# Dilated heads first, larger first loads, a value copy that may go to ScalarE, and slot sums copied out in two parts

## The chip, the cores and the metric

The kernel runs on one core of a Trainium2 chip. Its engines are TensorE (PE, with weight loads shown apart as PEld), VectorE (DVE), ScalarE (ACT), GpSimd (POOL) and SyncE (SP); 16 DMA engines move data. The metric is the device time of one launch in microseconds. Three runs of the kernel before took 178.34, 179.11 and 179.09 us, a median of 179.09.

## The reference: what is computed

Attention over 8 batches, 8 heads, 576 positions and 64 features, then a soft mixture of 8 experts with 4 slots each, over the 4608 tokens of 512 features that attention gives. Heads 0 to 3 see a plain window, heads 4 to 7 a dilated one:

```python
scores = scale * np.matmul(q, k.transpose(0, 1, 3, 2))
rel = pos[:, None] - pos[None, :]
mask_plain = (rel >= 0) & (rel < 32)
mask_dil = (rel >= 0) & (rel < 128) & (rel % 4 == 0)
masks = [mask_plain if h < H // 2 else mask_dil for h in range(H)]
attn = softmax(where(masks, scores, -1e9)); out = attn @ v
# x: the tokens, 4608 x 512
logits = x @ phi                                   # 32 slots
d = exp(logits - max over tokens), normalized over tokens
slot_input = d.T @ x                               # 8 experts x 4 slots
h = np.maximum(slot_input[e] @ w1[e], 0.0); slot_out[e] = h @ w2[e]
c = exp(logits - max over slots), normalized over slots
result = c @ slot_out
```

All inputs and the result are float32 in HBM. The result has 9.4 MB; the inputs read have 61.9 MB.

## The kernel before, in words

**Units.** Attention is cut into 8 units. A unit is two batches and either the four plain heads or the four dilated ones; units 0, 2, 4, 6 are plain and units 1, 3, 5, 7 dilated (`ty = u % 2`). Units 2k and 2k+1 are the two halves of the heads of batches 2k and 2k+1.

**Loads.** POOL issues all loads, since they turn float32 into bfloat16. A unit's q, k and v go to one of three staging buffers `stg` (32 partitions each for q, k and v). A dilated unit takes three commands (L417), each row one piece of 9216 elements; a plain unit takes six (L424), each row two pieces of 4608 elements. The first unit is loaded in two halves (`load_first`, L438), each in six commands with pieces of 2304 elements, so that its first transposes need not wait for the whole. The load of unit u+3 waits until PE has transposed unit u out of its buffer. The weights of the first layer (`w1`) go to `WD` and one buffer of `stg`; those of the second (`w2`) go to the three `stg` buffers and then to `TT` when the last units are done with them. The last two to use `stg` (`wpair`, L806) are cut into row groups with tiny extra transfers (`mk`, L787) between them. The last weights (L473) are cut by halves of their 512 columns.

**A unit's stages.** `st_T` (L566): PE transposes q, k, v (plain: 144 of 64 rows by 96, L582; dilated: 72 of 128 rows by 96, L577) and ACT copies them to `TT` (L603). `st_S` (L610): PE computes scores (L621), ACT their exponentials into `PT` (L628), DVE multiplies by the mask (L636); six blocks. `st_V` (L639): PE turns v back (L646) and DVE copies it to `VN` (L651), four times. `st_P`: PE multiplies (L675), DVE takes the reciprocal of the sums (L684) and scales into `XB` (L686), four times. `st_X`: PE transposes `XB` (L703), DVE or ACT copies it to `XT` (L715, L716), whichever the planner finds free first.

**A pair's stage.** After the second unit of a pair, `st_L` does for each batch: logits (L730), their exponential with its sum over tokens `csum` (L735), re-ordered pieces `expX` (L742), a transpose by a selecting matrix (L761), its copy `ET` (L765), and the slot sums into a PSUM bank `psA` (L774).

**The end.** DVE copies `psA` out (L854); PE folds it in two parts of two blocks each (L861), which become `siT` (L869); then the first layer (L883), ReLU (L890, L893), transposes (L901) and their copies, the sums over slots (L930), and the second layer (L957), by column halves at its end as the weights land. Each half is scaled (`so_sb`, L991), multiplied with the tokens' weights (L1009, L1022), scaled and stored by SP in 256-column pieces for six groups; four larger groups (L1072) follow with all 512 columns.

**What sets the order.** Each operation is recorded with its inputs, an estimated cost and a due time (`key`); a planner (`schedule`) places them on the engines, each engine in order, and writes the semaphores. Where PE would idle, it inserts matmuls of ones (L1090), the fillers, by the table `FILL` (times, modes, slack). POOL's and SP's commands keep the order in which they were recorded.

Of the kernel before, what the change touches and what calls it, by code (L numbers as in the profile page):

```python
# [8 lines left out]
ACTF = mybir.ActivationFunctionType  # L9
# [10 lines left out]
CT = 72  # L20
NU = 8
QB = 96
HALO = 32
FILL = ((1.5, 9.0, "h", 0.4, 0.43), (9.5, 13.5, "h", 0.6, 0.25), (13.5, 116.0, "h", 0.3, 0.216),
        (13.5, 24.0, "rf", 0.3, 0.216), (116.0, 143.0, "hrfc", 0.15, 0.216))
# [280 lines left out]
def bass_dilated_sliding_attn__then__soft_moe_slots_kernel(  # L306
# [12 lines left out]
    op = P.op  # L319
# [7 lines left out]
    stg = sb("stg", [128, 3, 9216])  # L327
# [21 lines left out]
    psA_sb = sb("psA_sb", [128, DM], F32)  # L349
# [29 lines left out]
    def sbt(t):  # L379
        return t.pool.ts[t.phys[0]]  # L380
# [7 lines left out]
    def bankb(t):  # L388
        return psb[:, t.phys[0], :]
# [8 lines left out]
    b_id0, b_id, b_sel, b_fold, b_rowm, b_phist, b_phi = [Buf() for _ in range(7)]  # L398
    b_acc, b_psA, b_csum, b_rcs, b_rtok = [Buf() for _ in range(5)]
    b_expT, b_expX = [Buf() for _ in range(B)], Buf()  # L400
# [4 lines left out]
    def due(u, x):  # L405
        return u * PACE + x

    def load_unit(u):
        bp, ty, s = u // 2, u % 2, u % 3

# [21 lines left out]
    def load_first(h_):  # L432
        def f(g):
            res = []
            for t, src in enumerate((q, k, v)):
                for bpar in range(2):
                    rows = src[bpar].rearrange("h (p c) d -> (h p) (c d)", c=CT)[0:32]
                    res.append(g.dma_start(  # L438
                        stg[32 * t + bpar:32 * t + 32:2, 0, :].rearrange(
                            "r (x f) -> r x f", x=2)[:, :, 2304 * h_:2304 * h_ + 2304],  # L440
                        rows.rearrange("(x r) f -> r x f", x=2)[:, :, 2304 * h_:2304 * h_ + 2304]))
            return res
        op("pool", f, w=[b_half[h_]], cost=3.5, sem=DmaSem(nc, f"s_first{h_}"),
           nbytes=96 * 4608 * 4, ndma=6)

# [110 lines left out]
    def win(u, t, h01, i, bpar):  # L556

        if u % 2 == 0:
            base = (2 * t + h01) * S + QB * i
        else:  # L560
            base = (4 * t + 2 * (i // 3) + h01) * 288 + QB * (i % 3)
        base -= HALO if t else 0
        n = QB if t == 0 else 128
        return TT[:, u % 2, 2 * base + bpar:2 * (base + n - 1) + bpar + 1:2]

    def st_T(u, j):  # L566
        ty, s = u % 2, u % 3
        src = stg[0:96, s, :].rearrange("r (x c d) -> r x c d", x=2, c=CT)
# [41 lines left out]
    def st_S(u, i):  # L610
        ty = u % 2
        sc, pt = tile(psum, 2), tile(pPT)
# [26 lines left out]
    def st_V(u, g):  # L639
# [4 lines left out]
        def pe(t):  # L644
# [5 lines left out]
        op("pe", pe, r=[b_id, b_TT[u % 2]], w=[pv], alloc=[pv, vn], cost=0.35, key=k0)  # L650
        op("dve", lambda dv: dv.tensor_copy(  # L651
            sbt(vn)[:, :, :, 0:64],
            bankb(pv)[:, 0:768].rearrange("p (m x d) -> p m x d", m=6, x=2)),
           r=[pv], w=[vn], cost=0.47, key=k0 + 0.6)

    def st_P(u, g):
        bp, ty = u // 2, u % 2
        bpar, h01 = g // 2, g % 2
# [32 lines left out]
    def st_X(u, bpar, x):  # L691
        bp, ty = u // 2, u % 2
        b = 2 * bp + bpar
# [448 lines left out]
```

## Time and profile before

| what | us |
|---|---|
| median of three runs | 179.09 |
| profiled execution: span from its first to its last instruction | 176.3 |
| first loads land (first half of unit 0) | 9.34 |
| first scores begin on PE (L621) | 16.99 |
| last unit transposed, POOL goes on | 116.73 |
| slot sums copied out (L854) | 134.20 |
| last weights landed, last second-layer matmuls begin | 152.17 |

Busy shares of the span: PE 80%, PEld 58%, DVE 64%, ACT 53%, POOL 24%. The page gives the profiled execution's own time as its span alone; the timed runs include what lies around it.

The page's first part is busy time of each engine; its second part cuts the span into 40 slices of 4.4 us, with one digit for each (9 is 90% or more), and gives for DMA the mean busy share of the 16 DMA engines and the GB/s that they moved. GB/s counts what is written: a load that turns float32 into bfloat16 reads twice that. A table of stretches gives for each stretch its length, each engine's busy time with its number of instructions, the granted clock of PE, the DMA share and GB/s. The share can be above 1, since an engine may have two pieces under way. The chain that ended last is followed back from the last instruction to what released it; its lines give start, length and what ran. In the timeline the bracket at the end of a line tells how long the engine had idled and for what. A DMA issue's line ends with the time from the command to its landing, with all the time that it stood in the queue.

### The profile page before, as it was taken

The page shows a single profiled execution, that of the slowest core. Times are in us where ns is not written, and L with a number is a line of the kernel's source. Part 1 is how long each engine was busy: PE and PEld are TensorE (multiplying, and loading weights), DVE is VectorE, ACT ScalarE, POOL GpSimd, SP SyncE. Part 2 cuts the span into 40 slices and gives each one's busy share as a digit, 9 for nine tenths or more (in the row PEclk, how much of TensorE's full clock was granted, in tenths as well). Part 3 has the DMA queues.
Part 4 walks back from the last instruction along what each step waited for, and adds up shares of the span by engine and source line. Part 5 has one row for each costly group of instructions (what it writes and reads, how often), then busy time and mean ns, then how long its engine had stood idle before and what let it go on. Part 6 is the DMA issues. An engine that isn't in the chain of part 4 may idle for free.

```text
span 176.3 us, 5745 instructions
## 1 busy us (share of the span) xinstructions
PE 141.8 (80%) x2574; PEld 101.4 (58%) x2574; DVE 113.6 (64%) x264; ACT 93.3 (53%) x143; POOL 42.4 (24%) x80
## 2 busy tenths in 40 slices
PE   7689988797989889797988698889899997598000
PEld 2266677566778667576966676776556555352000
DVE  6830986992897699479589467869953023489200
ACT  2044867744767866665885467577240212599000
POOL 7997105202200800500200010059930000000000
PEclk9969999999999999999999789999999999969955
DMA  4999999998999999999999999999999999999997
GB/s 71 178 230 206 207 217 210 234 225 185 224 207 219 240 209 196 215 213 214 239 200 211 214 218 214 216 218 214 216 207 214 205 193 200 268 344 398 448 428 297
DMA packets 12712, 40.80 MB, mean 231 GB/s; under 512 B 2256, under 2 KB 8912, under 8 KB 9424
## 3 DMA queue, kind: packets, MB, share of 16 engines
q0 software_dynamic: 8272, 30.94, 87.9%
q1 hardware_dynamic: 4416, 9.50, 14.0%
q8 instruction: 20, 0.33, 0.7%
q14 instruction: 4, 0.03, 0.0%
HBM read 61.93 MB, written 9.44 MB: 405 GB/s over the span
## 4 chain that ended last, share of the span: by engine, by line
PE 36%; DVE 21%; DMA 17%; POOL 7%; ACT 7%; issue 4%; POOLq 0%; DVEq 0%
DMA TT<-in_moe_w_dram 13%; PE ps L582 8%; DVE PT L636 6%; DVE XB L686 6%; PE ps L577 5%; ACT PT L628 4%; PE ps L703 4%; PE ps L730 4%; DVE VN L651 3%; DMA stg<-in_v_dram 3%; PE ps L646 3%; PE ps L621 3%; DVE WD L991 3%; PE ps L675 2%; PE ps L1090 2%
## 5 line engine op out<-in xcount | busy, mean ns | idle before, releaser
L603 ACT ACTIVATE TT<-ps 128x864 f32<-128x864 f32 x32 | 28.6, 896 | 28.4 <-PE ps L582 19.4
L628 ACT ACTIVATE PT<-ps 128x768 bf16<-128x768 f32 x48 | 36.7, 814 | 8.5 <-PE ps L621 8.4
L686 DVE TENSOR_TENSOR XB<-ps,RV 96x768 bf16<-96x768 f32 x32 | 30.3, 947 | 0.6
L651 DVE COPY VN<-ps 128x768 bf16<-128x768 bf16 x32 | 17.5, 546 | 6.4 <-PE ps L646 6.2
L1090 PE MATMUL ps<-wrm 128*128 128x512 bf16 x60 | 19.7, 458 | 1.1 <-DVE wrm L490 1.1
L582 PE MATMUL ps<-ident,stg 96*64 96x96 bf16 x576 | 16.5, 216 | 4.1 <-DMA stg<-in_v_dram 2.0
L715 DVE COPY XT<-ps 128x576 bf16<-128x576 bf16 x19 | 11.4, 598 | 12.8 <-PE ps L703 12.6
L675 PE MATMUL ps<-VN,PT 128*128 128x65 bf16 x384 | 17.8, 194 | 1.5 <-DVE PT L636 0.8
L582 PEld LDWEIGHTS ps<-ident,stg 96*64 96x64 bf16 x576 | 14.3, 116 | 7.6 <-DMA stg<-in_v_dram 2.6
L703 PE MATMUL ps<-ident,XB 96*128 96x96 bf16 x192 | 13.2, 207 | 4.9 <-DVE XB L686 2.9
L675 PEld LDWEIGHTS ps<-VN,PT 128*128 128x128 bf16 x384 | 14.5, 98 | 3.8 <-DVE PT L636 1.6
L646 PE MATMUL ps<-ident,TT 128*128 128x128 bf16 x192 | 16.0, 221 | 0.6 <-DVE VN L651 0.4
L621 PE MATMUL ps<-TT 64*128 64x96 bf16 x384 | 14.9, 204 | 1.2 <-ACT PT L628 0.9
L577 PE MATMUL ps<-ident,stg 96*128 96x96 bf16 x288 | 15.0, 206 | 0.5 <-DVE XB L686 0.3
L992 ACT ACTIVATE WD<-ps,rtok 128x256 f32<-128x256 f32 (+1 forms) x22 | 10.2, 559 | 8.4 <-PE ps L1009 8.2
L703 PEld LDWEIGHTS ps<-ident,XB 96*128 96x128 bf16 x192 | 9.7, 98 | 8.3 <-DVE XB L686 5.2
L577 PEld LDWEIGHTS ps<-ident,stg 96*128 96x128 bf16 x288 | 13.1, 98 | 0.7 <-DVE XB L686 0.4
L636 DVE TENSOR_TENSOR PT<-PT,mask_d 128x768 bf16<-128x768 bf16 x24 | 12.9, 546 | 0.7 <-ACT PT L628 0.2
L646 PEld LDWEIGHTS ps<-ident,TT 128*128 128x128 bf16 x192 | 10.8, 98 | 4.2 <-issue 1.3
L621 PEld LDWEIGHTS ps<-TT 64*128 64x128 bf16 x384 | 9.5, 94 | 5.8 <-ACT PT L628 2.3
L636 DVE TENSOR_TENSOR PT<-PT,mask_p 128x768 bf16<-128x768 bf16 x24 | 12.7, 539 | 0.1
L730 PE MATMUL ps<-XT,phi_pad 128*128 128x192 bf16 (+1 forms) x64 | 10.3, 306 | 1.6 <-issue 1.3
(95 smaller groups left out, 183.4 us busy)
## 6 DMA issues: line engine op xcount, KB each, us to landing
WD<-in_moe_w_dram POOLq DMA_DIRECT2D x7, 1024.0 KB, 30.6
stg<-in_moe_w_dram POOLq DMA_DIRECT2D x5, 1024.0 KB, 25.6
stg<-in_q_dram POOLq DMA_DIRECT2D x4, 576.0 KB, 22.0
stg<-in_k_dram POOLq DMA_DIRECT2D x4, 576.0 KB, 24.0
stg<-in_v_dram POOLq DMA_DIRECT2D x4, 576.0 KB, 26.8
out_dram<-WD SPq DMA_DIRECT2D x9, 256.0 KB, 2.8
out_dram<-WD SPq DMA_DIRECT2D x2, 1024.0 KB, 5.7
out_dram<-WD SPq DMA_DIRECT2D x1, 2048.0 KB, 9.2
```

The lines of the kernel that those rows point to most:

```text
L577: i_ = t.transpose(bankb2(pt, a)[:, 96 * kk:96 * kk + 96], two[:, c, :], ident[0:96, 0:96])
L582: i_ = t.transpose(bankb2(pt, a)[64 * hx:64 * hx + 64, 96 * kk:96 * kk + 96], src[:, hx, c, :], ident[0:96, 0:96])
L603: return ac.activation(d, sv, ACTF.Copy)
L621: i_ = t.matmul(pair(sc)[:, hx, QB * x:QB * x + QB], win(u, 1, h01, blk_, bpar)[64 * hx:64 * hx + 64], win(u, 0, h01, blk_, bpar)[64 * hx: ...
L628: op("act", lambda ac: ac.activation(sbt(pt)[:, 0:768].rearrange("p (x n) -> p x n", x=2), pair(sc)[:, :, 0:384], ACTF.Exp, scale=SCALE), ...
L636: return dv.tensor_tensor(p_, p_, m.unsqueeze(1).to_broadcast([128, 2, 384]), AluOp.mult)
L646: i_ = t.transpose(bankb(pv)[:, 128 * m:128 * m + 128], win(u, 2, h01, m, bpar), ident[:, :])
L651: op("dve", lambda dv: dv.tensor_copy(sbt(vn)[:, :, :, 0:64], bankb(pv)[:, 0:768].rearrange("p (m x d) -> p m x d", m=6, x=2)), r=[pv], w= ...
L675: i_ = t.matmul(pair(po)[:, bk, 65 * po_:65 * po_ + 65], sbt(pts[i])[:, o_:o_ + 128], sbt(vn)[:, m, half, 0:65], start=True, stop=True)
L686: op("dve", lambda dv: dv.tensor_tensor(sbt(xb)[:].rearrange("p m (x h d) -> p h x m d", x=2, h=2)[:, h01], pv()[:, :, :, 0:64], sbt(rv)[: ...
L703: i_ = t.transpose(bankb(px)[:, QB * m:QB * m + QB], sbt(xb)[:, m, 128 * x:128 * x + 128], ident[0:QB, 0:QB])
L1090: i_ = te.matmul(bank(t).rearrange("p (a x) -> p a x", a=4), wrm[:], wrm[:].unsqueeze(1).to_broadcast([128, 4, 128]), start=True, stop=True)
```

## The change

Four edits. First, a new function `kind(u)` makes units 0, 2, 4, 6 dilated and 1, 3, 5, 7 plain, and replaces `u % 2` wherever that chose the kind of heads. Second, the first unit is therefore dilated; its two halves take three commands each, a row being one piece of 4608 elements. Third, the planner may put each of the last unit's four copies of v on DVE or ACT. Fourth, the slot sums are copied out of PSUM by two DVE instructions, each with the two blocks that one fold reads, and each fold waits for its own part. The fillers' table also allows fillers before transposes of the dilated form (mode "f") at the start.

In the order of instructions that the planner makes of it, one of the last unit's four copies goes to ACT; of the `XT` copies 17 are on DVE and 15 on ACT (19 and 13 before). PE's first row of fillers is 14 long instead of 15, then 36 transposes, 8 fillers, 36 transposes, 4 fillers (before: 72, 7, 72, 4). POOL issues the first halves in 3 + 3 commands, then unit 1 in 6 and unit 2 in 3; SP's order is the same.

```diff
-FILL = ((1.5, 9.0, "h", 0.4, 0.43), (9.5, 13.5, "h", 0.6, 0.25), (13.5, 116.0, "h", 0.3, 0.216),
+FILL = ((1.5, 9.0, "hf", 0.4, 0.43), (9.5, 13.5, "hf", 0.6, 0.25), (13.5, 116.0, "h", 0.3, 0.216),
...
+    def kind(u):
+        return 1 - u % 2
+
     def load_unit(u):
-        bp, ty, s = u // 2, u % 2, u % 3
+        bp, ty, s = u // 2, kind(u), u % 3
...
             for t, src in enumerate((q, k, v)):
-                for bpar in range(2):
-                    rows = src[bpar].rearrange("h (p c) d -> (h p) (c d)", c=CT)[0:32]
-                    res.append(g.dma_start(
-                        stg[32 * t + bpar:32 * t + 32:2, 0, :].rearrange(
-                            "r (x f) -> r x f", x=2)[:, :, 2304 * h_:2304 * h_ + 2304],
-                        rows.rearrange("(x r) f -> r x f", x=2)[:, :, 2304 * h_:2304 * h_ + 2304]))
+                rows = src[0:2].rearrange("b h (p c) d -> b (h p) (c d)", c=CT)[:, 32:64]
+                rows = rows.rearrange("b (r x) f -> r b x f", x=2)[:, :, h_]
+                res.append(g.dma_start(
+                    stg[32 * t:32 * t + 32, 0, 4608 * h_:4608 * h_ + 4608], rows))
             return res
-        op("pool", f, w=[b_half[h_]], cost=3.5, sem=DmaSem(nc, f"s_first{h_}"),
-           nbytes=96 * 4608 * 4, ndma=6)
+        op("pool", f, w=[b_half[h_]], cost=1.75, sem=DmaSem(nc, f"s_first{h_}"),
+           nbytes=96 * 4608 * 4, ndma=3)
...
-        op("dve", lambda dv: dv.tensor_copy(
-            sbt(vn)[:, :, :, 0:64],
-            bankb(pv)[:, 0:768].rearrange("p (m x d) -> p m x d", m=6, x=2)),
-           r=[pv], w=[vn], cost=0.47, key=k0 + 0.6)
+        def ev(en):
+            d_, s_ = sbt(vn)[:, :, :, 0:64], bankb(pv)[:, 0:768].rearrange(
+                "p (m x d) -> p m x d", m=6, x=2)
+            return en.tensor_copy(d_, s_) if en is nc.vector else en.activation(d_, s_, ACTF.Copy)
+        op(("dve", "act") if u == NU - 1 else "dve", ev, r=[pv], w=[vn],
+           cost={"dve": 0.47, "act": 0.7}, key=k0 + 0.6)
...
-    op("dve", lambda vv: vv.tensor_copy(psA_sb[:], psA), r=[b_acc, t_acc], w=[b_psA], cost=0.65, key=K1)
+    b_psA2 = [Buf(), Buf()]
+    for y in range(2):
+        def ev(en, y=y):
+            d_, s_ = [a.rearrange("p (s c) -> p s c", c=4)[:, :, 2 * y:2 * y + 2] for a in (psA_sb[:], psA)]
+            return en.tensor_copy(d_, s_)
+        op("dve", ev, r=[b_acc, t_acc], w=[b_psA2[y]], cost=0.4, key=K1 - 1 + 0.1 * y)
...
-        op("pe", pe_f, r=[b_psA, b_fold], w=[fo], alloc=[fo], cost=1.0, key=K1 - 0.5 + 0.1 * y)
+        op("pe", pe_f, r=[b_psA2[y], b_fold], w=[fo], alloc=[fo], cost=1.0, key=K1 - 0.5 + 0.1 * y)
```

The same swap of `u % 2` for `kind(u)` is made in `win`, `st_T`, `st_S`, `st_P` and `st_X`.

More of the change, by code (lines that the diff above doesn't have):

```diff
@@ L398, in bass_dilated_sliding_attn__then__soft_moe_slots_kernel @@
     b_id0, b_id, b_sel, b_fold, b_rowm, b_phist, b_phi = [Buf() for _ in range(7)]
-    b_acc, b_psA, b_csum, b_rcs, b_rtok = [Buf() for _ in range(5)]
+    b_acc, b_csum, b_rcs, b_rtok = [Buf() for _ in range(4)]
     b_expT, b_expX = [Buf() for _ in range(B)], Buf()
@@ L556, in win @@
     def win(u, t, h01, i, bpar):
-        if u % 2 == 0:
+        if kind(u) == 0:
             base = (2 * t + h01) * S + QB * i
@@ L566, in st_T @@
     def st_T(u, j):
-        ty, s = u % 2, u % 3
+        ty, s = kind(u), u % 3
         src = stg[0:96, s, :].rearrange("r (x c d) -> r x c d", x=2, c=CT)
@@ L610, in st_S @@
     def st_S(u, i):
-        ty = u % 2
+        ty = kind(u)
         sc, pt = tile(psum, 2), tile(pPT)
@@ L650, in st_V @@
         op("pe", pe, r=[b_id, b_TT[u % 2]], w=[pv], alloc=[pv, vn], cost=0.35, key=k0)
-        op("dve", lambda dv: dv.tensor_copy(
-            sbt(vn)[:, :, :, 0:64],
-            bankb(pv)[:, 0:768].rearrange("p (m x d) -> p m x d", m=6, x=2)),
-           r=[pv], w=[vn], cost=0.47, key=k0 + 0.6)
+        def ev(en):
[4 more added lines that the diff above has]
+           cost={"dve": 0.47, "act": 0.7}, key=k0 + 0.6)
     def st_P(u, g):
-        bp, ty = u // 2, u % 2
+        bp, ty = u // 2, kind(u)
         bpar, h01 = g // 2, g % 2
@@ L691, in st_X @@
     def st_X(u, bpar, x):
-        bp, ty = u // 2, u % 2
+        bp, ty = u // 2, kind(u)
         b = 2 * bp + bpar
```

## The prediction

> **What bounds the kernel now.** I read the page's strip of DMA busy time first, then the DMA queues, then a table of stretches, then the chain that ended last, and at its end the timeline. From the page:
>
> ```profile
> span 176.3 us, 5745 instructions
> DMA  4999999998999999999999999999999999999997
> ...
> q0 software_dynamic: 8272, 30.94, 87.9%
> ```
>
> The DMA engines are busy in every slice but the first and the last. Queue q0 holds POOL's loads (q, k, v and the expert weights, turned from float32 to bfloat16 on the way). The table of stretches, its last two columns the DMA share and GB/s:
>
> ```profile
> 2.50:3.50 1.00, 1.00 (x4) 0.34 (x3) 0.58 (x6) 0.00 (x0) 1.00 (x4) 1.00 0.81 83
> 3.50:9.50 6.00, 4.01 (x16) 1.33 (x16) 5.06 (x20) 0.26 (x1) 5.94 (x13) 1.00 1.03 179
> 9.50:12.00 2.50, 2.50 (x74) 2.11 (x73) 0.42 (x2) 1.21 (x2) 2.43 (x3) 0.67 1.06 210
> 44.00:60.00 16.00, 14.51 (x325) 12.17 (x324) 12.27 (x27) 11.51 (x18) 3.24 (x7) 1.00 1.03 216
> 152.00:153.00 1.00, 0.29 (x4) 0.10 (x4) 0.48 (x1) 0.00 (x0) 0.00 (x0) 1.00 0.72 248
> 160.00:175.50 15.50, 2.34 (x8) 0.63 (x7) 4.29 (x7) 3.45 (x6) 0.00 (x0) 0.74 1.00 417
> ```
>
> From 9.5 us on loads flow at a full share. Only the start is slow: 83 GB/s, then 179, against 210 later. After 160 us the stores alone fill the engines, while PE, DVE and ACT have nearly stopped. The chain that ended last, in order of time:
>
> ```profile
> 3.96 5.38 DMA stg<-in_v_dram
> ...
> 116.44 0.28 issue
> 116.73 0.59 POOL stg L806
> ...
> 128.41 23.72 DMA TT<-in_moe_w_dram
> ...
> 152.17 0.32 PE ps L957 x4
> ```
>
> This chain runs through PE up to 116.7 us, then through POOL's commands, then through one transfer of 23.7 us. That is misleading: a command that takes 21 us to land was mostly standing in the queue. Two lines tell how deep the queue is where POOL had just waited for PE (the waits, and the issues between 115 and 130 us):
>
> ```profile
> POOL stg L806 <- PE ps L577: 14.4, 1, 14.4
> ```
> ```profile
> stg<-in_moe_w_dram POOLq DMA_DIRECT2D x1, 512.0 KB, 13.6
> ```
>
> POOL sat 14.4 us until the last unit's transposes freed its staging buffer, yet the first load issued then (512 KB) landed 13.6 us later. At about 213 GB/s it needs 2.5 us itself, so some 11 us of older work lay ahead of it, and PE could have been that much later without a gap in the stream. PE at the end of the loads, from the timeline:
>
> ```profile
> 147.37 0.29 PE L957 MATMUL ps<-TT,hT 128*32 128x256 bf16 x4 [0.38 <-DMA TT<-in_moe_w_dram]
> 150.70 0.29 PE L957 MATMUL ps<-TT,hT 128*32 128x256 bf16 x4 [0.20 <-DMA TT<-in_moe_w_dram]
> 152.17 0.29 PE L957 MATMUL ps<-TT,hT 128*32 128x256 bf16 x4 [1.18 <-DMA TT<-in_moe_w_dram]
> ```
>
> At each of the last pieces of the second weights PE waits for the load: 0.4, 0.2 and 1.2 us. So the bound is the load stream to 152.2 us and then the stores, 24.1 us more to the span's end. What moves the end of the load stream moves the end; what only moves PE, ACT or DVE by less than these waits does not.
>
> The sum is made against the span of the profile, 176.3 us; the median of the timed runs, 179.09, is 2.8 above it. I take the same shift for both. About 0.5% (0.9 us) is what a measurement of this kernel can tell from no change.
>
> **The change, part by part.**
>
> *First unit's loads.* Removed: 12 POOL commands of 144 KB, 505 to 640 ns each, 12 x 0.53 = 6.3 us of POOL. Added: 6 of 288 KB; the nearest row, the dilated load (L417, 519 ns), gives about 3.2 us. The bytes are the same, 1.77 MB written, in pieces of 9,216 bytes instead of 4,608. POOL's order behind it: unit 1 is now plain (6 commands, 3.1 us, instead of 3), then the mask selects, then unit 2 dilated (3 instead of 6). By sums the selects end near 10.7 us instead of 11.5; the first mask product starts only at 18.3, so nobody waits. SP's queue keeps its order.
>
> What the stream gains: in 3.5 to 9.5 us it lost (210 - 179)/210 x 6 = 0.9 us, in 2.5 to 3.5 (210 - 83)/210 x 1 = 0.6 us. The larger pieces and fewer commands can take away at most both, 1.5 us; at least nothing, because the stretch 9.5 to 12 shows the same small pieces at 210 GB/s, so size alone is no brake. The first microsecond is the start of 16 engines and stays. Of the 0.9 I take two thirds, 0.6: pieces and commands are halved, so a loss per piece or per command halves, and twice the bytes per command also fill the queue sooner. Both ends, 0 and -1.5, are kept for the range. A loss here I exclude: the plain loads of later units use these pieces, and the stream holds 206 GB/s or more wherever they flow.
>
> *One unit's pieces.* With the order swapped, one dilated unit moves from 18,432-byte pieces to 9,216 (four plain units now use the 9,216 form, three did). Between 12.5 and 20 us, mostly large pieces, q0 moved 1.65 MB at a share of 104.2%; between 20.5 and 28, mostly middle ones, 1.56 MB at 100.3%. Per share that is 211 against 207 GB/s, 2% of the 8.4 us that a unit takes: +0.17 us. Ends 0 and +0.3.
>
> *Unit order on PE, ACT and DVE.* The first unit needs 72 transposes of 128 rows instead of 144 of 64 rows; 18 of the former take 0.77 us on the chain, 36 of the latter 0.89, so the four groups differ by 4 x 0.12 = 0.5 us. The first half should land some 0.5 us before 9.34, so the first scores (16.99) start about 1 us earlier. The last unit gets the slower transposes, which releases POOL's L806 up to 0.5 us later: nothing against 11 us of queue. The last unit's XT copies on DVE cost 0.46 us (plain) instead of 0.75. All of it lies beside the load stream; worth 0. Without that cover it would be about -1.3 us.
>
> *Value copies.* In the order of instructions one of the last unit's four goes to ACT, behind two of its exponentials, with three masks' worth of work (four exponentials, 0.81 us each) queued behind it. DVE loses 0.55 us in a stretch where it is nearly full; ACT gains something between the XT copy of 576 columns (0.65) and the TT copy of 864 (0.90), by width 0.8. On the path this would be -0.55 to +0.8; it ends near 122 us, PE waits for loads at 147, so 0.
>
> *Slot sums.* The copy of 0.69 us becomes two of about 0.48 (the nearest 128x256 DVE row, L991). The first fold can start 0.2 us earlier; the second copy lies beside the first fold's half of 2.04 us. Ends -0.3 to +0.3, the second if the halves' stride costs double. PE has 0.4 us of waiting at 147.37 to swallow either: 0.
>
> Sum: -0.6 + 0.17 = -0.4 us. Span 175.9, time 178.7.
>
> [...] In 3.5 to 9.5 us DVE was busy 5.06 of 6 us, nearly all of it filling buffers; it stopped at 9.2 us and the rate went to 210 in the next row. [...]
>
> **The rivals.**
>
> *B, the whole start is cured.* The ramp shortens too, because each of the first commands brings twice the bytes. For it: a command brings 144 KB per 0.53 us, 280 GB/s, little above the stream's own rate, so the queue fills slowly. Against it: the DMA share in 3.5 to 9.5 is already 1.03, so engines were not empty, only slow. Then -1.5 + 0.17 = -1.3: 177.8.
>
> *C, the start stays as slow.* The loss goes by time, with whatever ran until 9.2 us, and not by piece. For it: the recovery at 9.5 with the same pieces. Against it: POOL's commands in that time also halve for this unit. Then +0.17: 179.3. [...]
>
> *D, slower: PE becomes last.* The logits and slot sums of a finished pair (L730 to L774) rode in the plain stages, which took 15.3, 14.7 and 15.0 us from scores to scores; they now ride in the dilated ones, 13.6 and 15.4 without them. Their DVE part is 4 x 0.22 + 2 x 0.53 = 1.9 us per pair. If the dilated stages grow by it and the plain ones, 12.5 us without it at the start, don't shrink, three pairs cost 5.8 us; the head and tail of PE gain about 1.5, and 1.2 is covered by the wait at 152.17: +3.1, 182.2. It decides once PE is over 1.2 us late at the last piece, that is once the pairs cost 2.7. Against it: the plain stages have the same work to lose, and DVE is busy only 10.4 of 13.6 us in a dilated stage.
>
> **How the numbers follow.** A (the forecast) 0.44, B 0.28, C 0.16, D 0.12. Time 178.7 by A, whose own range is 178.2 to 179.2 with the spread of runs taken in. For 8 in 10: D is left out at the top, which leaves room for 0.08 below; from B's -1.5 end with the 0.4 us that runs differ, 177.3, up to C with the pieces' upper end and the same 0.4 and some of D, 180.0. Faster by over 0.5%: B and a fifth of A, 0.37; slower: D, 0.12; the rest, 0.51, within.
>
> **What would show it.** In the changed profile: L441's six commands of 288 KB; the stretch 3.5 to 9.5 us at about 195 GB/s (B: 210 with the first microsecond over 120; C: 180); the last piece of the loads at 151.8 instead of 152.17, PE still waiting there; from there 24 us to the end as before. If PE shows no wait before its last L957 group, D is right. Gaps in the DMA strip between 10 and 150 us would make the whole frame wrong.

## The result and the profile after

The changed kernel takes 179.05 us in the median (178.35 to 181.21, 16 runs); the kernel before, beside it, 178.73 us (177.93 to 179.44, 16 runs). The ratio is 1.0042, 95% interval 1.0023 to 1.0062: 0.75 us, or 0.4%, slower; the medians differ by 0.32 us. The forecast was 178.7, 0.4 us faster than before. The time lies inside the range, and the difference is under the 0.5% that the prediction set as its bound of "no change", but its sign is the other one, and its interval does not reach zero. The ratios leave out executions over 1.5% above the fastest of their kernel, one of the 16 here but eight of 12 in a later experiment (e10), so medians of all executions stand beside the ratios.

The profiled execution of the changed kernel took 178.83 us, its span is 177.1. Every execution here takes about 1.75 us more than its span, so that the profiled execution of before (span 176.3) stands for some 178.0 us, not for the 179.09 with which the prediction paired it.

The page of the changed kernel, its granted clock and DMA strips (40 slices of 4.4 us) and its load queue:

```profile
span 177.1 us, 5739 instructions
...
PEclk9958999999999969999969999999999999999655
DMA  5999999999999999999999999999999999699996
...
q0 software_dynamic: 8128, 30.94, 87.1%
```

The same bytes are loaded, in 144 packets fewer. New are two things: the clock strip has two dips in the middle (slices 15 and 21, at 62 and 90 us) where before had one, and the DMA strip has a 6 at 150 us, the place where the loads hand over to the stores. The table of stretches at the start of the changed kernel (last columns: granted clock, DMA share, GB/s):

```profile
2.50:3.50 1.00, 1.00 (x4) 0.34 (x3) 0.58 (x6) 0.06 (x1) 0.93 (x4) 1.00 1.10 120
3.50:9.50 6.00, 3.25 (x18) 1.52 (x17) 5.31 (x20) 0.20 (x1) 5.93 (x11) 0.89 0.97 197
9.50:12.00 2.50, 2.50 (x31) 2.34 (x30) 1.74 (x11) 0.96 (x2) 2.50 (x5) 0.50 1.06 221
```

The start of the stream is faster, 120 for 83 GB/s and 197 for 179. Its last packet lands at 151.07 us, in the trace of before at 151.82. The same table where the loads end, of the kernel before (whose row from 152 to 153 us the prediction shows) and then of the changed one:

```profile
150.00:152.00 2.00, 0.79 (x9) 0.30 (x6) 0.41 (x1) 1.24 (x4) 0.00 (x0) 1.00 1.04 233
...
153.00:160.00 7.00, 6.91 (x29) 3.78 (x30) 5.66 (x10) 6.44 (x14) 0.00 (x0) 0.76 1.02 345
```
```profile
150.00:152.00 2.00, 1.58 (x18) 0.82 (x16) 1.30 (x3) 1.92 (x6) 0.00 (x0) 1.00 0.52 122
152.00:153.00 1.00, 0.67 (x7) 0.61 (x7) 0.51 (x2) 0.35 (x1) 0.00 (x0) 1.00 0.82 271
153.00:160.00 7.00, 6.84 (x30) 2.69 (x28) 7.00 (x12) 7.00 (x16) 0.00 (x0) 1.00 0.97 323
```

Half of the DMA engines' time between 150 and 152 us goes unused: the loads are nearly through and the first stores only begin at 150.60 (before: 149.94). Counted as share times length from 150 us to the end, before used 25.43 of 26.3 us (2.08 + 0.72 + 7.14, and 0.95 x 16.3 after 160), the changed kernel 24.90 of 27.1 (1.04 + 0.82 + 6.79, and 0.95 x 17.1). The work left after 150 us fell by 0.53, the unused time grew by 1.33, and the difference, 0.80, is that of the spans. Why the stores are late stands in PE's timeline at the end of the loads:

```profile
147.73 0.60 PE L966 MATMUL ps<-TT,hT 128*32 128x512 bf16 x7
148.93 0.39 PE L1018 MATMUL ps<-so_sb,expT 128*128 128x256 bf16 x2 [0.60 <-DVE so_sb L1000]
...
150.35 0.94 PE L966 MATMUL ps<-TT,hT 128*32 128x256 bf16 x10
151.44 0.29 PE L966 MATMUL ps<-TT,hT 128*32 128x256 bf16 x4 [0.16 <-DMA TT<-in_moe_w_dram]
```

L966 is before's L957. PE reaches the first half of the last weights without a wait, where it had waited 0.38 us before, and waits 0.16 us, not 1.18, for the last piece. PE and the loads now end together. The slot sums are copied out at 135.69 us, before at 134.20. This 1.5 us comes from the first scores (17.75 instead of 16.99, when 1 us earlier was forecast), the first unit's stage (0.7 longer), and the last unit's (16.7 instead of 16.0 us from its first exponentials); the three pairs between them differ by 0.6 the other way. The first unit's stage now carries the 144 transposes of the plain unit behind it (293 matmuls, before 223), and in the last unit's PE stands still for 0.91 us at 120.4 us with nothing that it waits for, which before does not have there. The head, in PE's timeline:

```profile
8.83 3.06 PE L578 MATMUL ps<-ident,stg 96*128 96x96 bf16 x36 [2.75 <-DMA stg<-in_v_dram]
11.69 3.52 PE L1099 MATMUL ps<-wrm 128*128 128x512 bf16 x8
15.04 1.70 PE L578 MATMUL ps<-ident,stg 96*128 96x96 bf16 x36
```

PE's fillers ran out 2.75 us ahead of the first load, the clock was halved from 8.2 to 15.0 us (10.4 to 13.8 before), and the 36 transposes priced at 2 x 0.77 us took 3.06.

### The profile page after: what moved, and what is told of

It reads as the page before. It is cut to its first block, busy times and chain, and to the rows that moved or that the text cites. A ratio compares the mean times of both kernels' runs of the same rounds, so it can differ in the third digit from the quotient of the medians.

```text
span 177.1 us, 5739 instructions
## 1 busy us (share of the span) xinstructions
PE 140.3 (79%) x2567; PEld 102.6 (58%) x2568; DVE 112.5 (64%) x262; ACT 94.8 (54%) x146; POOL 40.9 (23%) x77
## 4 chain that ended last, share of the span: by engine, by line
PE 35%; DVE 26%; DMA 16%; POOL 6%; issue 4%; ACT 3%; POOLq 0%; DVEq 0%
DMA TT<-in_moe_w_dram 12%; PE ps L583 8%; DVE PT L637 8%; DVE XB L690 6%; PE ps L578 6%; DVE VN L656 5%; PE ps L707 4%; PE ps L647 4%; DMA stg<-in_v_dram 4%; PE ps L734 4%; DVE WD L1000 3%; PE ps L622 3%; PE ps L679 3%; POOL TT L474 2%; POOL stg L810 2%
## 5 line engine op out<-in xcount | busy, mean ns | idle before, releaser
L656 DVE COPY VN<-ps 128x768 bf16<-128x768 bf16 x31 | 17.1, 550 | 11.7 <-PE ps L647 11.7
L578 PE MATMUL ps<-ident,stg 96*128 96x96 bf16 x288 | 15.9, 215 | 3.4 <-DMA stg<-in_v_dram 2.7
L622 PE MATMUL ps<-TT 64*128 64x96 bf16 x384 | 16.5, 214 | 2.5 <-issue 0.9
L1099 PE MATMUL ps<-wrm 128*128 128x512 bf16 x54 | 17.4, 455 | 1.1 <-DVE wrm L491 1.1
L583 PE MATMUL ps<-ident,stg 96*64 96x96 bf16 x576 | 15.8, 207 | 2.7 <-issue 2.5
L719 DVE COPY XT<-ps 128x576 bf16<-128x576 bf16 x17 | 10.1, 595 | 11.2 <-PE ps L707 11.2
L578 PEld LDWEIGHTS ps<-ident,stg 96*128 96x128 bf16 x288 | 14.2, 103 | 4.9 <-DMA stg<-in_v_dram 3.2
L647 PE MATMUL ps<-ident,TT 128*128 128x128 bf16 x192 | 17.0, 230 | 0.0
L583 PEld LDWEIGHTS ps<-ident,stg 96*64 96x64 bf16 x576 | 13.4, 110 | 4.2 <-issue 2.7
L622 PEld LDWEIGHTS ps<-TT 64*128 64x128 bf16 x384 | 10.4, 99 | 7.3 <-ACT PT L629 1.5
L647 PEld LDWEIGHTS ps<-ident,TT 128*128 128x128 bf16 x192 | 11.9, 104 | 3.0 <-issue 0.6
L720 ACT ACTIVATE XT<-ps 128x576 bf16<-128x576 bf16 x15 | 9.7, 648 | 5.4 <-PE ps L707 5.4
```

The lines of the kernel that those rows point to most:

```text
L578: i_ = t.transpose(bankb2(pt, a)[:, 96 * kk:96 * kk + 96], two[:, c, :], ident[0:96, 0:96])
L583: i_ = t.transpose(bankb2(pt, a)[64 * hx:64 * hx + 64, 96 * kk:96 * kk + 96], src[:, hx, c, :], ident[0:96, 0:96])
L622: i_ = t.matmul(pair(sc)[:, hx, QB * x:QB * x + QB], win(u, 1, h01, blk_, bpar)[64 * hx:64 * hx + 64], win(u, 0, h01, blk_, bpar)[64 * hx: ...
L647: i_ = t.transpose(bankb(pv)[:, 128 * m:128 * m + 128], win(u, 2, h01, m, bpar), ident[:, :])
L656: return en.tensor_copy(d_, s_) if en is nc.vector else en.activation(d_, s_, ACTF.Copy)
L1099: i_ = te.matmul(bank(t).rearrange("p (a x) -> p a x", a=4), wrm[:], wrm[:].unsqueeze(1).to_broadcast([128, 4, 128]), start=True, stop=True)
```

## The experiments

Two questions: is the load term right, and who took it back? The ratios are against the kernel before, run beside each.

**The head and its fillers.** In e1 and e2 the second row of the fillers' table is removed, in e1 from the changed kernel, in e2 from the one before:

```diff
-FILL = ((1.5, 9.0, "hf", 0.4, 0.43), (9.5, 13.5, "hf", 0.6, 0.25), (13.5, 116.0, "h", 0.3, 0.216),
+FILL = ((1.5, 9.0, "hf", 0.4, 0.43), (13.5, 116.0, "h", 0.3, 0.216),
```

> The changed kernel without the eight fillers between the two halves of the first unit's transposes (the row of the fillers' table for 9.5 to 13.5 us is taken out; nothing else). Theory P (the loads end 0.7 us earlier, but PE is now last: its scores begin 0.8 us later and the slot sums are copied out 1.5 us later than before): the first scores come 2 to 3 us earlier than 17.75, the first so_sb waits for a load again (near 147.5), the DMA engines idle under 0.5 us between 150 and 153, and the time is 0.7 to 1.2 us under the changed kernel, 0.996 to 0.998 of the kernel before. Theory S (the swap of pieces or the stores cost the time, and PE is not last): 1.004 as the changed kernel, whatever PE does.

> The kernel before without the seven fillers at the same place. Theory P: loads are last there, PE has only 0.4 us of waiting to lose, so 0.997 to 1.001 of the kernel before. Theory S: 1.000. If it gains as much as the first run does over the changed kernel, PE was already last before and the chain of loads was misread.

e1: 182.18 us, ratio 1.0192 [1.0145, 1.0238]; slot sums at 138.1, loads still through at 151.1, stores from 152.94. What was expected, that the head would gain, failed. It is the plainest evidence against the prediction's frame: with the loads where they were, PE 2.4 us later than in the changed kernel cost 2.7 us more by the ratios. e2: ratio 1.0003 [0.9983, 1.0022] at slot sums 132.2. The kernel before does not care.

e5 goes the other way: in the changed kernel 24 head fillers instead of 14, so that PE works up to the first load (granted clock 1.00 from 2.5 to 12 us).

```diff
-FILL = ((1.5, 9.0, "hf", 0.4, 0.43),
+FILL = ((1.5, 9.0, "hf", 0.4, 0.262),
```

> The changed kernel with 24 fillers instead of 14 before its first transposes, so that PE works until the first half lands and its granted clock shouldn't fall to a half there. Theory G (what makes PE late are periods of half clock, 13.6 us of them by the slot sums in the changed kernel against 6.8 before): no half clock before 20 us, first exponentials 1 to 2 us earlier than 18.1, slot sums near 134 instead of 135.7, time 0.996 to 1.001 of the kernel before. Theory O (the order itself: logits beside dilated stages and a plain unit last): the first exponentials come as early, but the way from them to the slot sums stays at 117.5 us or grows, time 1.002 or more.

The first exponentials start at 16.3 us instead of 18.1, and it helps nothing: slot sums at 138.6 in the profiled execution (180.97 us), 180.37 us in the median, ratio 1.0026 [0.9990, 1.0062]. The way from the first exponentials to the slot sums grew from 117.5 to 122 us, as theory O had it. A good head is not enough; PE loses its time later.

**The size of the first loads.** e3 cuts the changed kernel's first loads into 12 commands with pieces half as long, as before had them:

```diff
-                res.append(g.dma_start(
-                    stg[32 * t:32 * t + 32, 0, 4608 * h_:4608 * h_ + 4608], rows))
+                for y in range(2):
+                    res.append(g.dma_start(
+                        stg[32 * t:32 * t + 32, 0, 4608 * h_ + 2304 * y:4608 * h_ + 2304 * y + 2304],
+                        rows[:, :, 2304 * y:2304 * y + 2304]))
```

> The changed kernel with its first unit loaded in twelve commands of pieces half as long, as the kernel before has them. Theory P: the loads end some 0.7 us later, near 151.8, PE is as late as in the changed kernel, so the time is that of the changed kernel or up to 0.4 us more: 1.003 to 1.007. Theory S with the pieces at fault: back to 1.000.

3.5 to 9.5 us runs at 176 GB/s again (194 in e5 and 197 in the changed kernel, which have the larger pieces), the loads end at 152.27, and the time is 180.06 us, ratio 1.0043 [1.0011, 1.0075]. The rate at the start follows the pieces or the commands, which e3 changes together; in this order of units it does not reach the end by the ratios (1.0043 and 1.0042).

**The copies.** e4 makes only the two copy edits (a value copy on ScalarE, slot sums in two parts) in the kernel before.

> The kernel before with the value copies of the last unit on VectorE or ScalarE and the slot sums copied in two parts; order of heads and first loads as before. Theory P: both edits shift PE by under 0.5 us beside the load stream, 0.998 to 1.002. If one of them is what made PE late, the slot sums come over 0.5 us later than 134.2 and the time is 1.003 or more.

178.74 us, ratio 1.0005 [0.9982, 1.0029]: worth nothing, as forecast.

**One pair in the new order.** e7 is the changed kernel with only units 0 and 1 swapped; e8 adds the 24 head fillers.

```diff
-        return 1 - u % 2
+        return 1 - u % 2 if u < 2 else u % 2
```

> The changed kernel with the dilated heads first in the first pair of units alone; the other three pairs are plain first again, so the logits ride in plain stages and the last unit is dilated. First loads as in the changed kernel. Theory O: the stages are as short as before, slot sums near 134 to 134.5, loads end near 151.1, time 0.996 to 0.999 of the kernel before. Theory G: as many half-clock periods as fall by chance of the waits, mainly the one at 8 to 15 us; slot sums 134.5 to 136, time 0.999 to 1.004.

> The run before with 24 fillers ahead of the first transposes. If G and O each hold in part, this takes both away: first exponentials near 16.5, slot sums at 133 or earlier, PE waits for the last weights again, loads end near 151.1, time 0.994 to 0.997 of the kernel before. If it is no faster than the kernel before, the end is set by something else than PE and the loads.

e7: ratio 0.9998 [0.9970, 1.0027], median 179.28, slot sums at 135.9. That is what theory G had; theory O's 134 to 134.5 and its gain did not come. e8: 0.9947 [0.9918, 0.9977], median 178.41, inside the range expected; its profile is of an execution of 180.99 us with the slot sums at 138.6, so the early slot sums are not shown. With the later pairs as before, the larger first loads can pay once the head has 24 fillers. The medians, 0.6 us above and 0.3 below that of the kernel before beside them (178.68), say so less clearly.

**The first unit loaded whole.** These take the head out of the question: unit 0 is loaded at once and PE works on fillers (35) until all of it is there. e6 is the kernel before so changed, e9 too but with its own 12 small commands, e10 is the changed kernel, and e11 is e6 with the two copy edits. e10 and e11 thus differ in the order of units alone, and in the form of the first unit's loads that follows from it.

```diff
-    load_first(0)
+    load_unit(0)
...
-    load_first(1)
...
-        o = op("pe", pe, r=[b_id, b_stg[s] if u else b_half[j // 2]], w=[pt], alloc=[pt],
+        o = op("pe", pe, r=[b_id, b_stg[s]], w=[pt], alloc=[pt],
```

> The kernel before, plain heads first, with its first unit loaded at once in six commands of pieces of 4608 elements instead of two halves of pieces of 2304, and 35 fillers in the wait before it; no other edit. It is the gain of larger first pieces without the order. All theories with the loads as the bound: loads end 0.5 to 0.9 us earlier than 151.8. G and O both: PE starts its transposes near 11.5 us and has its scores near 17 as before, slot sums near 134, so the time follows the loads: 0.995 to 0.999. If it is 1.000, PE was already as much a bound before.

> The control of e6: the kernel before, whose first transposes wait for both halves of the first unit, with the same 35 fillers before them, but loaded in its own twelve commands of pieces of 2304 elements. If e6's gain came from larger pieces, the loads end at 151.8 again and the time is 0.999 to 1.002 of the kernel before. If it came from PE, kept busy through the wait and in one stretch of transposes, the time is near e6's 0.993.

> The changed kernel with its first unit loaded at once in three commands and 35 fillers before its transposes. Loads as early as in e6. Theory O or G through the order (dilated first makes PE late): slot sums 135.5 or later, time 0.998 to 1.006 of the kernel before and 0.5 to 1.2% over e6, with a wide spread. If it is as fast as e6, 0.993, the order costs nothing and only the head of the changed kernel (halves, fillers, half clock) was at fault.

> e6 with the two other edits of the change, value copies on VectorE or ScalarE and slot sums in two parts. From e4, where they changed nothing, 0.990 to 0.996. Over 0.998: they make PE late where PE is close to being last.

| run | order | median us | ratio | slot sums copied out | loads end | stores begin |
|---|---|---|---|---|---|---|
| e6 | plain first | 177.24 | 0.9927 [0.9898, 0.9956] | 136.1 | 151.77 | 151.30 |
| e9 | plain first | 177.87 | 0.9951 [0.9927, 0.9975] | 134.0 | 151.74 | 150.12 |
| e11 | plain first | 177.26 | 0.9935 [0.9914, 0.9956] | 132.8 | 151.28 | 149.57 |
| e10 | dilated first | 181.81 | 1.0042 [1.0003, 1.0080] | 139.5 | 151.56 | 154.38 |

(e6's profile is of an execution of 178.76 us, 1.5 above its median; e10's, 181.87, is near its median.) With the head alike and the loads ending within 0.3 us of each other, the order costs 4.5 us in the median and 1.9 us by the ratios (e10 against e11). e6 gained more than was expected of it. e9 gained two thirds as much, with loads that end as late as those of before: by the terms set for it, most of the gain is not that of larger pieces. In e10's profile the DMA engines run dry between the loads and the stores:

```profile
150.00:152.00 2.00, 2.00 (x36) 1.23 (x29) 0.00 (x0) 0.00 (x0) 0.00 (x0) 1.00 0.34 49
152.00:153.00 1.00, 0.40 (x5) 0.27 (x4) 0.48 (x1) 0.00 (x0) 0.00 (x0) 1.00 0.00 0
```

**How late PE may be.** e12 puts 12 matmuls of ones, 2.6 us, ahead of the first fold in the kernel before.

```diff
+            for _ in range(12 if y == 0 else 0):
+                t.matmul(bank(fo).rearrange("p (a x) -> p a x", a=4), wrm[:],
+                         wrm[:].unsqueeze(1).to_broadcast([128, 4, 128]), start=True, stop=True)
```

> The kernel before with twelve extra matmuls of ones, 2.6 us at full clock, on PE just before the slot sums are folded; loads untouched. It prices a late PE. By the waits for loads in the trace of before, 0.4 us at the first half of the second layer and 1.2 us at its last piece, a lateness of 2.6 us should cost 1.4 to 2.2 us: 1.008 to 1.012 of the kernel before. Theory S, with PE hidden: 1.000.

178.57 us, ratio 0.9975 [0.9950, 1.0000]. The second layer starts 2.2 us later (145.43 for 143.24) and it costs nothing in the median, where 1.4 to 2.2 us were expected, though the profiled execution, 1.0 us longer than that of before, already has a share of 0.77 between 150 and 152 us. PE's cover is thus, by estimate from these numbers, about 2 us. Beside that PE waits only 0.28 us for the last loads (before 0.38, 0.20 and 1.18), and the half clock that before has from 153.7 us is gone. With the slot sums at 135.7 the changed kernel's profile is at the edge of that cover; e10's, at 139.5, is well past it. One thing stays open here: against the end of its loads, PE starts the second layer equally late in e12 (6.7 us ahead of it) and in the changed kernel (6.6; before, 8.6), yet only the changed kernel is slower by the ratio. Its executions also spread more, 178.35 to 181.21 us against 177.39 to 179.13.

**Which part of the order.** e13 and e14 write each filler as four matmuls of 128 columns, which moves all later matmuls some 80 places along in PE's program; e15 and e16 turn the last pair alone back or round.

```diff
-                i_ = te.matmul(bank(t).rearrange("p (a x) -> p a x", a=4), wrm[:],
-                               wrm[:].unsqueeze(1).to_broadcast([128, 4, 128]), start=True, stop=True)
+                for x in range(4):
+                    i_ = te.matmul(bank(t)[:, 128 * x:128 * x + 128], wrm[:], wrm[:], start=True, stop=True)
```

> Changed kernel with each 512-column filler matmul written as four of 128 columns: the same filler columns, but some 80 matmuls more ahead of the first scores, so that every later matmul stands about 0.6 of the spacing of 127 matmuls further along in PE's program. Theory H (what the order costs comes from stalls of 1 to 2 us that recur every 127 matmuls and, in this order, fall where PE is emptiest, each followed by 3.4 us of half clock): the stalls move to other places of the stages, the half-clock periods near 62.8 and 90.1 us go or move, the slot sums are copied out at 134.5 instead of 135.7, and the ratio to the kernel before is 0.997 to 1.000. Theory C (the content of the stages in this order costs it): the slot sums stay at 135.5 to 136.5, ratio 1.003 to 1.006.

> Kernel before with the same shift of PE's program. Theory H: the stalls leave their present places here too, and the kernel before can lose what it had by luck: up to 2 us on PE, slot sums at 135 to 136, ratio 1.000 to 1.004. Theory C: nothing changes but the head: slot sums at 134 to 134.5, ratio 0.998 to 1.002.

e13: 181.13 us, ratio 1.0103 [1.0061, 1.0145], slot sums at 138.9. e14: 178.01 us, ratio 0.9985 [0.9959, 1.0010], slot sums at 133.7. The shift did not mend the changed kernel, which came out slower than either theory had it, and it did not hurt the kernel before. That speaks against chance places (theory H), but not against the stalls themselves: e13 still has 1.4, 1.9 and 1.8 us of them (58.2, 90.6 and 117.7 us), each in a stage that carries logits.

```diff
-        return 1 - u % 2
+        return 1 - u % 2 if u < 6 else u % 2
```

(e15, on the changed kernel; e16 swaps `u < 6` the other way in the kernel before.)

> Changed kernel, dilated heads first in the first three pairs and plain heads first in the last pair, so that the last unit is dilated as in the kernel before. Theory T (the last unit costs it: 16.7 us from its first exponentials to the copy of the slot sums instead of 16.0): slot sums 0.7 us earlier, near 135.0, stores begin at 150.0, ratio 0.998 to 1.000. Theory M (the middle of the kernel costs it: half clock after stalls near 62.8 and 90.1): slot sums at 135.5 to 136.5, ratio 1.003 to 1.006.

> Kernel before with dilated heads first in its last pair alone; loads, head and the other three pairs as before. Theory T: the last unit takes 0.7 us more, slot sums at 134.9, stores begin at 150.6, ratio 1.002 to 1.005. Theory M: slot sums at 134.2 to 134.6 and ratio 0.998 to 1.002, since the first three pairs keep their order.

e15: 180.23 us, ratio 1.0030 [1.0008, 1.0051], slot sums at 136.9. e16: 178.51 us, ratio 1.0001 [0.9986, 1.0017], slot sums at 133.7. The last unit being plain is not it (theory T falls); the first three pairs hold the cost.

**What the stages weigh.** The tables of stages, from one unit's first exponentials to the next one's (columns after the length: busy time and instructions of PE, PEld, DVE, ACT, POOL), first of the kernel before:

```profile
44.38:59.64 15.26, 13.77 (x310) 11.51 (x308) 11.72 (x27) 10.77 (x18) 2.50 (x6) 1.00 1.03 215
59.64:73.28 13.64, 11.47 (x266) 8.75 (x265) 10.50 (x21) 8.84 (x13) 4.30 (x9) 1.00 1.02 216
73.28:88.04 14.76, 13.55 (x313) 11.53 (x311) 11.81 (x27) 10.83 (x17) 1.07 (x2) 1.00 1.06 221
```

Of the changed kernel:

```profile
43.89:60.08 16.19, 14.62 (x369) 12.00 (x367) 12.13 (x27) 10.81 (x18) 3.58 (x8) 1.00 1.02 216
60.08:73.24 13.16, 10.92 (x207) 9.19 (x205) 10.23 (x21) 9.06 (x15) 2.05 (x5) 0.87 1.05 218
73.24:90.77 17.53, 14.67 (x365) 11.93 (x363) 11.97 (x27) 10.79 (x17) 3.80 (x8) 0.98 1.01 213
```

Before, a stage that carries a finished pair's logits and slot sums has 310 matmuls, and the next has 266. In the new order they are about 365 and 207. The reason is to be seen in the chain that ended last, here that of the changed kernel between 45 and 58 us (start, length, what ran):

```profile
45.45 1.09 PE ps L734 x8
...
52.79 0.89 PE ps L583 x36
...
57.49 0.89 PE ps L583 x36
```

The stage of a dilated unit also transposes the next unit, a plain one, with its 144 transposes (L583, four such rows from 52.79 us on), twice as many as a dilated unit needs. Before, they lay in the stages without logits (L734); now logits and 144 transposes share one stage. e17 and e18 take 72 of the 144 away, for every plain unit but a first one, in e10 and in e11; that is four units in e17 and three in e18.

```diff
                     c = 18 * j + 9 * a + kk
+                    if u:
+                        i_ = t.transpose(bankb2(pt, a)[:, 96 * kk:96 * kk + 96],
+                                         two[:, c, :], ident[0:96, 0:96])
+                        continue
```

> Changed order, first unit loaded whole, and every later plain unit transposed by 72 matmuls of the dilated form instead of 144 of 64 rows; this leaves the plain heads' transposes wrong and so the result, while planner, order, loads and the work of the other engines stay. Theory W (weight of stages: in the changed order the stage that carries a finished pair's logits and slot sums also carries the next plain unit's 144 transposes, 365 matmuls and 14.4 to 14.8 us of PE work, and the stage after it has 210 and 11.1): the heavy stages of 16.5 to 17.5 us fall to 15 to 15.5, the slot sums are copied out at 133 to 135.5 instead of 139.5, half-clock periods near 31, 65 and 92 us are fewer, the ratio is 0.993 to 0.998. Theory Z (something else in the order costs it, as the half clock that starts the plain units or ACT's work): heavy stages stay above 16 us, slot sums at 137.5 or later, ratio 1.000 or more.

> The same cut of transposes in the order of before, first unit loaded whole, with the value copies and slot sum parts (the counterpart of e17). Theory W: here the plain unit's transposes lie in the light stages (265 matmuls, 11.0 to 11.3 us of PE in 13.6 to 14), so the stages shorten by 0.3 to 1 us each, slot sums at 130.5 to 132.5 instead of 132.8, and the ratio stays at 0.991 to 0.995, since the loads bound it. Theory Z: the same numbers; so what tells is that e17 comes as near to this kernel as 1 us by W, and stays 3 us or more behind by Z.

e17: 177.48 us, ratio 0.9937 [0.9913, 0.9960], where e10 had 181.81 and 1.0042; slot sums at 131.4 instead of 139.5. e18: 177.03 us, ratio 0.9914 [0.9887, 0.9941], slot sums at 129.3. The stages of e10 and then of e17:

```profile
46.62:63.65 17.03, 14.37 (x364) 11.76 (x362) 12.35 (x27) 10.90 (x17) 4.25 (x9) 1.00 0.99 209
63.65:75.61 11.96, 11.05 (x210) 9.32 (x210) 9.97 (x20) 9.08 (x14) 1.38 (x3) 0.86 1.07 224
75.61:93.15 17.54, 14.80 (x364) 11.99 (x362) 11.88 (x27) 10.91 (x18) 3.77 (x8) 0.97 0.99 208
```
```profile
46.36:61.27 14.91, 14.01 (x296) 11.64 (x294) 12.14 (x27) 10.72 (x17) 3.49 (x8) 1.00 1.02 215
61.27:73.18 11.91, 10.12 (x208) 8.29 (x206) 10.16 (x21) 8.86 (x14) 2.15 (x5) 1.00 1.05 218
73.18:88.09 14.91, 13.91 (x296) 11.61 (x294) 11.98 (x27) 10.71 (x17) 3.78 (x8) 1.00 1.01 212
```

Taking 72 matmuls from each heavy stage shortens the three of them by 2.1, 2.6 and 1.4 us (the third, from 105.81 us in e10, is not among the rows) and brings the dilated order to 0.5 us of its counterpart (177.48 against 177.03) from 4.5 us behind, or by the ratios to 0.4 from 1.9. The times flatter this, since PE waits for the last weights again in both (1.04 us each): the slot sums, 6.7 us apart in e10 and e11, are still 2.2 us apart. Theory W holds as to the place: the order costs mainly because it puts the 144 transposes and the logits into the same stage.

It does not hold as to the size. The heavy stages shorten by more than PE's busy time in them (0.4 to 0.9 us). With about 365 matmuls PE also sat idle for 2.2 to 2.7 us in them, with some 290 for 0.9 to 1.5. Most of this difference is stalls in which PE waits for nothing that the profile shows ("issue"); in PE's timeline of e10 (its L619 computes scores, its L582 makes the 144 transposes):

```profile
63.31 0.31 PE L619 MATMUL ps<-TT 64*128 64x96 bf16 x6 [1.76 <-issue]
90.45 0.74 PE L582 MATMUL ps<-ident,stg 96*64 96x96 bf16 x26 [1.83 <-issue]
```

A third, of 0.88 us, lies in the third heavy stage; e17 has no such stall over 0.3 us in its whole trace. In e11, the order of before, stalls are nearly as long (1.65 us at 69.9 us, 1.43 at 96.4; in the kernel before itself 1.30 at 70.5 and 1.39 at 96.9), but these lie in the light stages, where the 144 transposes lie too. e18 has none left there, and these stages shorten by 2.1 and 1.6 us, where theory W expected 0.3 to 1. So e17 and e18 take away two things at once, PE's work and the stalls that come with the 144 transposes, and no run parts the two.

With PE late, the time goes with its granted clock; which of the two leads is not shown. The dilated order of e10 ran in 177.85 us where the granted clock was 0.971 and in 184.56 where it was 0.913; e11's times lie between 176.98 and 179.64 at clocks from 0.942 to 0.966.

Best of all kernels that compute everything are e6 and e11, plain heads first and the first unit loaded whole: 177.24 and 177.26 us, 0.7% faster than the kernel before.

## Why the prediction was right, and where it was wrong

- *What bounds the kernel.* Right for the kernel before: 2.6 us of extra PE work cost it nothing in the median (e12). "What only moves PE, ACT or DVE by less than these waits does not" was right as a sentence; what followed from it was not, as PE moved by more.
- *First unit's loads, -0.6.* The direction was right and the size about right; whether pieces or commands did it was not parted. 3.5 to 9.5 us ran at 197 GB/s, forecast about 195, and at 176 when the pieces were cut again (e3). Loads end at 151.47 us in the mean of seven profiles with the larger first pieces (the changed kernel, e1, e5, e7, e8, e13, e15) and at 151.94 in seven with the small ones in the order of before (before, e2, e4, e9, e12, e14, e16): 0.47 us earlier, where -0.6 and +0.17 gave 0.43. The two groups overlap, 151.07 to 152.23 and 151.72 to 152.37. The last piece was expected at 151.8 and came at 151.44. The first microsecond, which was to stay at 83 GB/s, rose to 120. Rival C is out, and B needed 210 GB/s. DVE's work did not set this rate alone: DVE was busy 5.31 of the 6 us, before 5.06, and the rate rose from 179 to 197 GB/s all the same.
- *Value copies and slot sums, 0 each.* Right (e4; e11 beside e6). The two slot sum copies took 0.42 us each, 0.48 were forecast.
- *Unit order on PE, ACT and DVE, "worth 0".* This is the step that failed, in three terms. The first scores were to "start about 1 us earlier": they came 0.76 later, since fewer fillers left PE idle for 2.75 us (1.99 before), and the transposes ran at half clock (8.2 to 15.0 us). The last unit's copies were to be cheaper (0.46 us instead of 0.75): its stage took 0.7 us longer. And the stages between were not weighed on PE at all: the sum of a pair's work stays the same, but 310 and 266 matmuls become about 365 and 207, and that pairing, with the stalls that come with the 144 transposes, costs 4.5 us in the median between e10 and e11 (1.9 by the ratios). "24 us to the end as before" became 25.7, with half the DMA engines' time unused from 150 to 152 us.
- *Rival D, PE becomes last (0.12).* It had the place, logits riding in the dilated stages, and its test: PE without a wait ahead of the last L957 group. The wait fell from 1.18 to 0.16 us. What it got wrong is the engine and the size. It priced the logits by DVE's 1.9 us a pair and set DVE's 10.4 of 13.6 us against itself; the weight was PE's, in the 144 transposes and the stalls with them. That its 182.2 us is near e10's 181.81 is chance, since its sum was made of DVE's work; the changed kernel stays at the edge of PE's cover in most of its runs.
- *The chances.* That the two times differ by less than 0.5% was the likeliest case. That faster stood at 0.37 and slower at 0.12 came from pricing the gain on the stream and taking PE's side as covered. That 178.7 lies 0.35 us from the measured time is in part luck: it was taken from a median of 179.09, while the kernel before ran in 178.73 beside the changed one.

Left open: how the 0.75 us divides between head, heavy stages, stalls and half clock. In the two profiles shown, the pairs took no longer after than before (87.7 and 88.3 us for three); the heavy stages show between matched kernels, 88.5 for e10 against 84.7 for e11, and in the mean of the profiles: 86.7 for the order of before (before, e2, e4, e6, e9, e11, e12, e14) and 88.9 for the new one (the changed kernel, e1, e3, e5, e10, e13). Why loading the first unit whole gains 0.5% even with the small pieces (e9) was not settled either; its profile has one half-clock period ahead of the stores, before has two and a third at 153.7 us. That third one may be the reason: e9 and e14 begin their stores and scale their second halves within 0.3 us of before's times but lack it, and there the DMA engines move 360 to 373 GB/s between 153 and 160 us, where before moves 343 to 347, and the span ends 0.6 us earlier.

## What to carry to other kernels

When the order of units changes, count for each stage which work of its neighbours rides in it, engine by engine: sums over a pair stay equal while the heavier stage grows past what the lighter one can give back. "Hidden under waits for loads" holds only up to the length of these waits, so measure that cover, by extra work as in e12, before an engine's side of a change is put at zero. A gain on the bounding stream is worth having only as long as the engine behind it can take it up: here 0.5 us earlier loads met a PE that was 1.5 us later.

## What the runs showed of the hardware

- In the changed kernel PE lost its clock without being idle throughout. Stretches in which it was busy for 1.60 and 2.06 of 3.4 us (86.7 and 59.4 us) were each followed by 3.4 us at half clock (not every such stretch is: PE was busy for 2.03 of the 3.4 us from 95.85 us and kept its clock):

```profile
86.70:90.10 3.40, 1.60 (x42) 1.49 (x42) 0.60 (x1) 0.98 (x2) 0.72 (x2) 1.00 1.04 215
90.10:93.50 3.40, 3.40 (x51) 2.74 (x50) 2.19 (x4) 2.83 (x4) 0.35 (x1) 0.50 1.02 214
```

  Ahead of the stores, each period of half clock in the profiles of before and of the changed kernel lasted 3.41 us, the one in the changed kernel's head 6.83 us. What sets the clock is not shown.
- PE stood still for 0.36 to 1.95 us with nothing in the profile that it waits for ("issue") five times in the profile of before and five times in that of the changed kernel, counting what is over 0.3 us; the longest, at 86.55 us in the changed kernel, is on the chain that ended last. Counted in matmuls from the start, these places are 349, 858, 986, 1495 and 2131 in the changed kernel and 604, 987, 1242, 1624 and 1752 in the kernel before: from one to the next there are 127 to 128 matmuls, or a multiple of that. Each of the two traces has 20 transfers of 16 KB in queue q8, whose kind the page gives as "instruction", one every 7 us in the mean, and each of the ten stalls ends 1.25 to 1.62 us after one of these has landed; for the stall at 86.55 us that is the one at 86.88, and PE goes on at 88.50. What PE waits for is not shown, as no run changes these transfers alone.
- Lateness was free in e12: with the second layer 2.2 us later (145.43 us for 143.24), PE waited 0.28 us in all for the last loads, and the half clock of before from 153.7 to 157.1 us was absent (granted clock 1.00 between 153 and 160 us, before 0.76). Whether that made up for the delay was not measured by itself.
